# A gated mix of two attentions: row maxima of both heads in one PSUM bank, with a SyncE no-op between the halves

## The chip, the cores and the metric

The kernel runs on one core of a Trainium2 chip. The time is that of the device in microseconds (us), from launch to end; lower is better. The kernel before takes 1559.06 us (median of 3 runs, 1557.29 to 1560.24). The engines are called PE (TensorE; its weight loads, PEld, are listed apart), DVE (VectorE), ACT (ScalarE), POOL (GpSimd) and SP (SyncE).

## What is computed

Both branches read the same x of 2048 positions and 512 features, and a gate mixes them. Branch A is a dilated local attention (32 heads of 16, each position looks at 8 positions, 2 apart). Branch B is a full attention with 32 query heads and one shared head of keys and values; it is where nearly all the work is.

```python
x = A_x
g = sigmoid((x * gate_w).sum(-1, keepdims=True))
...
# branch B
q = (x @ wq).reshape(B, S, 32, 16).transpose(0, 2, 1, 3)
k = x @ wk; v = x @ wv
scores = einsum("bhqd,bkd->bhqk", q, k) * 16 ** -0.5
p = softmax(scores, axis=-1)
o = einsum("bhqk,bkd->bhqd", p, v)
b = o.transpose(0, 2, 1, 3).reshape(B, S, 512) @ wo
...
return g * a + (1 - g) * b
```

## The kernel before

**Units and steps.** Branch B is cut into 32 units: 4 blocks of 512 queries by 8 groups of 4 heads (unit u is block u // 8, group u % 8). A unit's queries stand in `qst[u % 8]`, 128 rows by 2 by 512. Rows 0 to 63 hold one head of a pair, rows 64 to 127 the other (the code's `odd` or `b`), and the middle index is the pair (`pr`). A number is kept as a high and a low part, so a head fills 48 rows; rows 62 and 63 of each half are for a shift. The keys `kst` are laid out the same way. TensorE runs a matmul on one half of its rows beside one on the other half if each writes its own PSUM bank.

**Two passes over the scores.** The softmax needs each query's row maximum before the exponential.

- *Maxima* (`max_mm`, L251): 128 queries are the stationary operand, 512 keys the moving one, and VectorE takes the maximum over the keys into the unit's tile `mx`. `fill_pair` (L269) does both heads of a pair: two matmuls into the two banks of `pm` (`m2` in the code) and one reduction of 128x1024. `fill_one` (L278) does one head alone: one matmul into the single bank `ps` (`m1`) and one reduction of 128x512 (L285). A unit needs 64 head pieces of 512 keys. When the last is in, `filled` (L258) reduces `mx` twice more and transposes the result (`mt`), ScalarE makes its high part (`shift_a`), VectorE the low part (`shift_c`, the tile `ml`), and `shift_b` (L301) writes them to rows 62 and 63 of `qst` by eight small DMAs: all eight from SyncE while branch A's pieces last, four from SyncE and four from GpSimd after that.
- *Exponentials* (`exp_pair`, L311): 128 keys are stationary, 512 queries moving; both heads of a pair go to the two banks of `pe`, and ScalarE takes the exponential of 128x1024 (`pexp`, L318). There are two such bank pairs, `eb[0]` and `eb[1]`, one for each pair of heads. The shift rows make the subtraction of the maximum part of the matmul. `weighted` (L323) then multiplies by the values: four matmuls of 32 columns each (8 in the trace) accumulate in `po` over the unit's 16 key blocks.

**The main loop** (L737) has 512 steps, 16 a unit. In each it issues the two score pairs of this step, the weighted sum of the step before, and, as far as there is room, maxima of later units: a pair into `pm` between the two score pairs and a lone piece into `ps` behind the second (the list `order`, L752). At a unit's end `finish_a` (L334) transposes `po` on VectorE and hands the scaling to GpSimd.

**The order is written out by a planner.** All instructions are issued in program order. The code keeps modelled clocks (`clk`) of TensorE, ScalarE and VectorE with fixed costs (L42: 0.23 us for a matmul pair, 0.92 for an exponential, 1.14 and 0.61 for the reductions, 1.18 for a weighted sum) and the time at which each bank comes free (`free`). `fill_ready` (L559) issues a maxima piece only if its bank is free by that clock, 0.15 us of slack allowed. `pause` (L569) fills the exponentials' banks where a unit's maxima are short. `tasks` holds later work with a due time, `run_tasks` (L598) issues what is due. Branch A's GpSimd work comes from `run_pool` (L655) in pieces with due times, with its own list `hooks` for the few VectorE and ScalarE instructions that belong to them.

**Around it.** Ahead of the loop (to 316 us) come the projections, with maxima filled in between. Four times the loop stops for an output phase (`out_phase`, L512), the product with the output weights for a quarter of the positions; it interleaves maxima as well and stores by `out_store` (L494). SyncE does no computing. It issues the queries' loads (`stack`, L228), the shift rows, loads of weights and the output stores, in the order of the program.

Of the kernel before, what the change touches and what calls it, by code (L numbers as in the profile page):

```python
# [6 lines left out]
F32 = mybir.dt.float32  # L7
# [29 lines left out]
NB = 8  # L37
NS = NU * NJ
NF = 2 * NU * 2 * 4 * 4


T_R, T_LAT, T_EXP, T_RED2, T_RED1, T_W, T_LUMP, T_Q = 0.23, 0.20, 0.92, 1.14, 0.61, 1.18, 2.53, 3.2  # L42


@with_exitstack
def gated_mix_kernel(ctx, tc, xt, wa, wk, wq, wo_a, wo_b, out):
# [191 lines left out]
    half = []  # L238
    free = {"m2": 0.0, "m1": 0.0, "e0": 0.0, "e1": 0.0, "po": 0.0}
    tasks, shifted = [], set()  # L240

    def fillable():
        return bool(half) or bool(slots) and slots[0][0] < len(stacked) and stacked[slots[0][0]] <= clk["pe"]

    def unit_tile(v):
        if v not in mx:
            mx[v] = wp.tile([P, 2, 2, 4, 4], F32, name="mx", bufs=3)
            left[v] = NF // NU
        return mx[v]

    def max_mm(dst, v, pr, t, kc, odd):  # L251
        b = 64 * odd
        nc.tensor.matmul(dst, qst[v % NB][b:b + 62, pr, t * P:(t + 1) * P], kst[b:b + 62, kc * 512:(kc + 1) * 512], start=True, stop=True)  # L253

    def to_go():
        return 2 * len(slots) + len(half)

    def filled(v, n):  # L258
        left[v] -= n
        if not left[v]:  # L260
            ms = wp.tile([P, 2, 2, 8], F32, name="ms")
            m = mx.pop(v).rearrange("p b i t k -> p b (i t) k")
            for x in range(2):
                nc.vector.tensor_reduce(ms[:, :, x, :], m, AX.X, ALU.max)
            mt = wp.tile([P, 32], F32, name="mt")
            nc.vector.transpose(mt, ms.rearrange("p b x y -> p (b x y)"))
            tasks.append((after("dve", 0, 0.5) + 0.1, shift_a, (v, mt)))

    def fill_pair(dst, key):  # L269
        v, pr, t, kc = slots.pop(0)  # L270
        m = unit_tile(v)
        for odd in range(2):
            max_mm(dst[:, odd, :], v, pr, t, kc, odd)
        nc.vector.tensor_reduce(m[:, :, pr, t, kc], dst, AX.X, ALU.max)  # L274
        free[key] = after("dve", after("pe", 0, T_R) + T_LAT, T_RED2) + 0.08
        filled(v, 2)

    def fill_one(dst=m1, key="m1"):  # L278
        if not half:
            v, pr, t, kc = slots.pop(0)  # L280
            half.extend([(v, pr, t, kc, 0), (v, pr, t, kc, 1)])
        v, pr, t, kc, odd = half.pop(0)
        m = unit_tile(v)
        max_mm(dst, v, pr, t, kc, odd)
        nc.vector.tensor_reduce(m[:, odd, pr, t, kc:kc + 1], dst, AX.X, ALU.max)  # L285
        free[key] = after("dve", after("pe", 0, T_R) + T_LAT, T_RED1) + 0.08
        filled(v, 1)

    def shift_a(v, mt):
# [5 lines left out]

    def shift_c(v, mt, th, ml):
        nc.vector.scalar_tensor_tensor(ml, mt, mk[:, 5:6], th.bitcast(F32), op0=ALU.mult, op1=ALU.add)  # L297
        after("dve", 0, 0.2)
        shift_b(v, ml)

    def shift_b(v, ml):  # L301
        for b in range(2):
# [36 lines left out]
    def finish_b(u, tt, eng):  # L339
        qb, hg = divmod(u, NHG)  # L340
        rl = wp.tile([P, 4 * 4], F32, name="rl")
        nc.vector.reciprocal(rl, tt[:, :, 16])  # L342
        at = after("dve", clk["pe"] + T_LAT, 0.8)
# [215 lines left out]
    def fill_ready(key, slack):  # L559
        if fillable() and free[key] <= clk["pe"] + slack:  # L560
            clk["pe"] = max(clk["pe"], free[key])
            if key == "m1":
                fill_one()
            elif half and (not slots or half[0][0] < slots[0][0] or slots[0][0] >= len(stacked)):
                fill_one(m2[:, 0, :], "m2")
            elif slots:
                fill_pair(m2, "m2")

    def pause(most):  # L569
        n = 0  # L570
        while n < most and slots and fillable():
            key = min(("e0", "e1", "m2"), key=lambda k: free[k])
            clk["pe"] = max(clk["pe"], free[key])
            if half:
# [20 lines left out]
            mm()  # L595
        return post

    def run_tasks():  # L598
        for task in [t for t in tasks if t[0] <= clk["pe"]]:
            tasks.remove(task)  # L600
# [37 lines left out]
    split_x(3, nc.gpsimd)  # L638
    load_wa(0)

    hooks, pool, done = [], 0.0, set()
    QK, AV = 12500, 22500
    pieces = [("load", 0)]
    wos = []
# [10 lines left out]
    def run_pool():  # L655
        nonlocal pool
        now = clk["pe"] * 1e3
        while pieces and pool < now + 3000:
# [7 lines left out]
            if kind == "load":  # L666
                a_load(g)
                pool += 500 if g else 6000
            elif kind == "qk0":
                a_scores(g, 0)  # L670
                pool += QK
            elif kind == "qk1":
                a_scores(g, 1)
                pool += QK
                hooks.append((pool + 6000, a_max, g, "max"))
            elif kind == "sub":
                a_sub(g)
                pool += 800
                hooks.append((pool + 4000, a_exp, g, "exp"))
                hooks.append((pool + 6500, a_sum, g, "sum"))  # L680
# [7 lines left out]
        for h in sorted(hooks, key=lambda h: h[0]):  # L688
            if h[0] <= now:
                hooks.remove(h)  # L690
                h[1](h[2])
                done.add((h[3], h[2]))


    lumps += [("q", m) for m in range(2, 4 * NQB)]
# [41 lines left out]
    for s in range(NS + 1):  # L737
# [100 lines left out]
```

## Time and profile before

| | |
|---|---|
| median of 3 runs | 1559.06 us (1557.29 to 1560.24) |
| the profiled execution's own time | 1558.8 us |
| its span, first to last instruction | 1557.0 us |
| granted TensorE clock | 0.998 |
| first and last exponential of the main loop | 316 and 1545 us |

The rows of the profile read so: a group has its line, engine, operation, names of what is written and read, shapes and count, then busy us and the mean ns of one, then the engine's idle time before it and who ended it. A row of a timeline has start and duration in us, engine, line, operation, names, shapes and count; in square brackets idle time before it and what released it. L253 is `max_mm` wherever it is called from, so its rows are told apart by the bank: pm, ps, pe, po, or pl in the front. L316 is a score matmul, L318 an exponential, L326 a weighted sum. Matmuls overlap: their starts are exact, their ends are modelled, so distances are taken from start to start.

### The profile page before, as it was taken

What the parts mean: (1) busy time and instruction counts of PE and PEld (TensorE: products, weight loads), DVE (VectorE), ACT (ScalarE), POOL (GpSimd) and SP (SyncE); (2) the same over time, 40 slices, a digit from 0 to 9 for tenths busy, and PEclk for the clock granted to TensorE, in tenths of its full rate; (3) what the DMA queues carried; (4) which work ended last, traced back from release to release, by engine and by line L of the source; (5) the groups of instructions that cost most, each with busy time, mean ns of one, the idle gap of its engine ahead of it and who ended that gap; (6) DMA issues with size and microseconds to landing.
All of it is one profiled execution on the core that took longest, in us unless ns stands there. A gap on an engine that the chain in (4) does not pass through costs nothing.

```text
span 1557.0 us, 25703 instructions
## 1 busy us (share of the span) xinstructions
PE 1525.7 (98%) x10076; PEld 703.8 (45%) x10076; DVE 1335.8 (86%) x1667; ACT 1120.9 (72%) x1315; POOL 834.2 (54%) x1015
## 2 busy tenths in 40 slices
PE   8999999999999999999999999999999999999998
PEld 4677777733333333333333333363354336333532
DVE  6899999979888898888899889898898889888731
ACT  4223111189999899999989998939966993999676
POOL 7420897778987898889887885240031004000210
PEclk9999999999999999999999999999999999999999
DMA  7842312211011101211111010000000000000000
GB/s 240 261 141 90 120 62 91 99 59 41 21 49 49 56 19 50 65 47 34 50 49 56 20 48 12 22 28 12 12 19 21 12 2 29 2 2 1 2 1 27
DMA packets 42889, 78.61 MB, mean 50 GB/s; under 512 B 8544, under 2 KB 25024, under 8 KB 40720
## 3 DMA queue, kind: packets, MB, share of 16 engines
q1 hardware_dynamic: 20224, 35.56, 7.9%
q0 software_dynamic: 4640, 26.99, 5.0%
q10 hardware_dynamic: 17904, 14.42, 2.8%
q8 instruction: 79, 1.29, 0.3%
q14 instruction: 42, 0.34, 0.1%
HBM read 46.96 MB, written 29.45 MB: 49 GB/s over the span
## 4 chain that ended last, share of the span: by engine, by line
PE 82%; DVE 12%; ACT 4%; issue 1%; DMA 0%; DVEq 0%; POOL 0%; ACTq 0%
PE po L326 30%; PE pe L316 21%; PE pm L253 9%; PE ps L253 8%; DVE mx L274 7%; PE pe L529 5%; DVE mx L285 4%; ACT pexp L318 3%; PE pl L159 3%; PE pl L160 2%; PE pl L161 2%; PE pl L167 1%; PE pl L253 1%; DVE ml L297 0%; PE po L253 0%
## 5 line engine op out<-in xcount | busy, mean ns | idle before, releaser
L318 ACT ACTIVATE pexp<-pe 128x1024 f32<-128x1024 f32 x1022 | 989.2, 1022 | 105.2 <-PE pe L316 100.4
L274 DVE TENSOR_REDUCE mx<-pm 128x2 f32<-128x1024 f32 x610 | 743.9, 1219 | 144.3 <-PE pm L253 140.9
L326 PE MATMUL po<-pexp,vst 128*32 128x512 f32 x4088 | 545.3, 605 | 0.7 <-ACT pexp L318 0.6
L316 PE MATMUL pe<-qst,kst 64*128 64x512 f32 x2044 | 467.0, 452 | 11.1 <-ACT pexp L318 5.8
L316 PEld LDWEIGHTS pe<-qst,kst 64*128 64x128 f32 x2044 | 191.1, 184 | 518.4 <-ACT pexp L318 506.2
L285 DVE TENSOR_REDUCE mx<-ps 128x1 f32<-128x512 f32 x597 | 405.5, 679 | 0.0
L253 PE MATMUL pm<-kst,qst 62*128 62x512 f32 x1230 | 262.6, 417 | 0.8 <-DVE mx L274 0.2
L253 PE MATMUL ps<-kst,qst 62*128 62x512 f32 x597 | 242.6, 406 | 0.4
L381 POOL TENSOR_TENSOR pr<-aext 128x512 f32<-128x512 f32 x128 | 163.9, 1302 | 57.1 <-DMA aext<-ad 57.0
L326 PEld LDWEIGHTS po<-pexp,vst 128*32 128x32 f32 x4088 | 80.4, 108 | 176.4 <-issue 163.3
L206 ACT ACTIVATE stage<-pl 128x384 f32<-128x384 f32 x64 | 31.5, 492 | 165.3 <-PE pl L161 162.8
L426 POOL TENSOR_TENSOR oa<-oa,av 128x512 f32<-128x512 f32 x112 | 143.5, 1281 | 8.8
L346 POOL TENSOR_TENSOR rl<-rl,gate_t 128x16 f32<-128x16 f32 x31 | 6.8, 220 | 242.6 <-DVE rl L342 242.6
L253 PEld LDWEIGHTS pm<-kst,qst 62*128 62x128 f32 x1230 | 117.4, 186 | 41.4 <-DVE mx L274 17.2
L253 PEld LDWEIGHTS ps<-kst,qst 62*128 62x128 f32 x597 | 111.1, 186 | 30.4 <-DVE mx L285 22.3
L424 POOL TENSOR_TENSOR av<-aext,lg 128x512 f32<-128x512 f32 x112 | 118.9, 1061 | 7.5
L305 POOL DMA_DIRECT2D qst<-ml x48 | 27.3, 573 | 134.6 <-DVE ml L297 130.8
L159 PE MATMUL pl<-wah,xh 128*128 128x384 f32 (+1 forms) x256 | 93.7, 366 | 0.4 <-ACT stage L206 0.4
L274 DVE TENSOR_REDUCE mx<-pl 128x2 f32<-128x1024 f32 x75 | 91.1, 1215 | 0.0
L160 PE MATMUL pl<-wal,xh 128*128 128x384 f32 (+1 forms) x256 | 87.1, 340 | 0.0
L161 PE MATMUL pl<-wah,xl 128*128 128x384 f32 (+1 forms) x256 | 86.9, 339 | 0.0
L529 PE MATMUL pe<-woh,turned 64*128 64x512 f32 x496 | 84.3, 400 | 0.1
(124 smaller groups left out, 1204.4 us busy)
## 6 DMA issues: line engine op xcount, KB each, us to landing
aext<-ad POOLq DMA_DIRECT2D x16, 1440.0 KB, 6.2
qst<-qd SPq DMA_DIRECT2D x64, 192.0 KB
ad<-stage ACTq DMA_DIRECT2D x32, 384.0 KB
qd<-qhi SPq DMA_DIRECT2D x32, 256.0 KB
xraw<-xt SPq DMA_DIRECT2D x16, 256.0 KB
qd<-qlo SPq DMA_DIRECT2D x16, 256.0 KB
qst<-ml SPq DMA_DIRECT2D x208, 2.0 KB
out<-two SPq DMA_DIRECT2D x12, 256.0 KB
```

The costliest lines, as they stand in the source:

```text
L159: mms.append(lambda c=c: nc.tensor.matmul(out_ap, ah(c), bh(c), start=(c == 0), stop=False))
L160: mms.append(lambda c=c: nc.tensor.matmul(out_ap, ah(c), bl(c), start=False, stop=False))
L253: nc.tensor.matmul(dst, qst[v % NB][b:b + 62, pr, t * P:(t + 1) * P], kst[b:b + 62, kc * 512:(kc + 1) * 512], start=True, stop=True)
L274: nc.vector.tensor_reduce(m[:, :, pr, t, kc], dst, AX.X, ALU.max)
L285: nc.vector.tensor_reduce(m[:, odd, pr, t, kc:kc + 1], dst, AX.X, ALU.max)
L316: nc.tensor.matmul(bank[:, odd, :], kst[b:b + 64, kt * P:(kt + 1) * P], qst[u % NB][b:b + 64, pr, :], start=True, stop=True)
L318: nc.scalar.activation(e, bank, AF.Exp, scale=SCALE)
L326: nc.tensor.matmul(po[32 * i:32 * i + 32, :], vst[:, kt, :], pexp[s, i // 2][:, i % 2, :], start=(kt == 0), stop=(kt == NJ - 1))
L381: nc.gpsimd.tensor_mul(pr[:, k], q, e[:, o:o + NJ, AC:2 * AC])
L424: nc.gpsimd.tensor_mul(av, e[:, o:o + NJ, 2 * AC:].rearrange("p j (h d) -> p j h d", d=DH), lg[:, w].unsqueeze(3).to_broadcast([P, NJ, AG, ...
L426: nc.gpsimd.tensor_add(ao, ao, av)
L529: nc.tensor.matmul(eb[x % 2][:, b, :], st[h], mv[h], start=first, stop=last)
```

## The change

- `fill_two` takes the place of `fill_one` in the main loop. It takes 256 keys for both heads of a pair (`quarter`, half of a slot). The odd head's matmul of 256 columns goes to the upper half of the bank `m1`, then SyncE gets a no-op that reads that half, then the step's two score pairs are issued, then the even head's matmul to the lower half. The second half is ordered behind the no-op, and the no-op behind the first half. One reduction of 128x512 takes both heads' maxima.
- The maxima tile has 8 columns of 256 keys where it had 4 of 512; `fill_pair` and `fill_one` reduce to two columns per head.
- The pair into `m2` is issued behind both score pairs, no longer between them, with 0.9 us of slack where there was 0.15.
- A leftover half slot goes to a free bank pair by `fill_apart`.
- The last reductions of a unit (`close`) become a task, `shift_b` a task of its own behind `shift_c`, and branch A's hooks become tasks. In the main loop at most one of the small VectorE tasks is issued per step, and none if VectorE's modelled clock is over 0.6 us ahead of TensorE's.
- `out_store` issues its store from GpSimd in place of SyncE. The planner's costs change in three places (1.18 to 1.21 for a weighted sum, 0.8 to 0.96 for `finish_a`, a new 0.14 for a 256-column pair); `mx` has two buffers, not three.

```diff
@@ -235,43 +236,45 @@
...
-            mx[v] = wp.tile([P, 2, 2, 4, 4], F32, name="mx", bufs=3)
+            mx[v] = wp.tile([P, 2, 2, 4, 8], F32, name="mx", bufs=2)
...
-    def max_mm(dst, v, pr, t, kc, odd):
-        b = 64 * odd
-        nc.tensor.matmul(dst, qst[v % NB][b:b + 62, pr, t * P:(t + 1) * P], kst[b:b + 62, kc * 512:(kc + 1) * 512], start=True, stop=True)
+    def max_mm(dst, v, pr, t, kc, odd, k=0, n=512):
+        b, k = 64 * odd, 512 * kc + k
+        nc.tensor.matmul(dst, qst[v % NB][b:b + 62, pr, t * P:(t + 1) * P], kst[b:b + 62, k:k + n], start=True, stop=True)
...
     def filled(v, n):
         left[v] -= n
         if not left[v]:
-            ms = wp.tile([P, 2, 2, 8], F32, name="ms")
-            m = mx.pop(v).rearrange("p b i t k -> p b (i t) k")
-            for x in range(2):
-                nc.vector.tensor_reduce(ms[:, :, x, :], m, AX.X, ALU.max)
-            mt = wp.tile([P, 32], F32, name="mt")
-            nc.vector.transpose(mt, ms.rearrange("p b x y -> p (b x y)"))
-            tasks.append((after("dve", 0, 0.5) + 0.1, shift_a, (v, mt)))
+            tasks.append((clk["dve"], close, (v, mx.pop(v).rearrange("p b i t k -> p b (i t) k"))))
+
+    def close(v, m):
+        ms = wp.tile([P, 2, 2, 8], F32, name="ms")
+        for x in range(2):
+            nc.vector.tensor_reduce(ms[:, :, x, :], m, AX.X, ALU.max)
+        mt = wp.tile([P, 32], F32, name="mt")
+        nc.vector.transpose(mt, ms.rearrange("p b x y -> p (b x y)"))
+        tasks.append((after("dve", clk["pe"], 0.66) + 0.1, shift_a, (v, mt)))
...
     def fill_pair(dst, key):
...
-        nc.vector.tensor_reduce(m[:, :, pr, t, kc], dst, AX.X, ALU.max)
+        nc.vector.tensor_reduce(m[:, :, pr, t, 2 * kc:2 * kc + 2], dst.rearrange("p o (h n) -> p o h n", h=2), AX.X, ALU.max)
...
@@ -282,8 +285,33 @@
...
+        nc.vector.tensor_reduce(m[:, odd, pr, t, 2 * kc:2 * kc + 2], dst.rearrange("p (h n) -> p h n", h=2), AX.X, ALU.max)
...
+        filled(v, 1)
+
+    def fill_two(between):
+
+        if not quarter:
+            v, pr, t, kc = slots.pop(0)
+            quarter.extend([(v, pr, t, kc, 0), (v, pr, t, kc, 1)])
+        v, pr, t, kc, h = quarter.pop(0)
+        m = unit_tile(v)
+        max_mm(m1[:, 256:512], v, pr, t, kc, 1, 256 * h, 256)
+        nc.sync.keepalive_nop([nc.sync.lower_ap(m1[:, 256:512])])
+        between()
+        max_mm(m1[:, 0:256], v, pr, t, kc, 0, 256 * h, 256)
+        nc.vector.tensor_reduce(m[:, :, pr, t, 2 * kc + h], m1.rearrange("p (o n) -> p o n", o=2), AX.X, ALU.max)
+        free["m1"] = after("dve", after("pe", 0, T_Z) + T_LAT, T_RED1) + 0.08
+        filled(v, 1)
+
+    def fill_apart(bank, key):
+
+        v, pr, t, kc, h = quarter.pop(0)
+        m = unit_tile(v)
+        for odd in range(2):
+            max_mm(bank[:, odd, 0:256], v, pr, t, kc, odd, 256 * h, 256)
+        nc.vector.tensor_reduce(m[:, :, pr, t, 2 * kc + h], bank[:, :, 0:256], AX.X, ALU.max)
+        free[key] = after("dve", after("pe", 0, T_Z) + T_LAT, T_RED1) + 0.08
...
@@ -295,8 +323,7 @@
 
     def shift_c(v, mt, th, ml):
         nc.vector.scalar_tensor_tensor(ml, mt, mk[:, 5:6], th.bitcast(F32), op0=ALU.mult, op1=ALU.add)
-        after("dve", 0, 0.2)
-        shift_b(v, ml)
+        tasks.append((after("dve", clk["pe"], 0.45) + 0.5, shift_b, (v, ml)))
 
@@ -498,7 +525,7 @@
         free[f"e{k}"] = after("act", clk["pe"] + T_LAT, 0.92)
         if n == C:
             nc.gpsimd.tensor_add(two[:, 0], two[:, 0], two[:, 1])
-            nc.sync.dma_start(out[0].rearrange("(p j) d -> p j d", j=NJ)[:, j, :], two[:, 0])
+            nc.gpsimd.dma_start(out[0].rearrange("(p j) d -> p j d", j=NJ)[:, j, :], two[:, 0])
         else:
             x = len(parts)
             if x < 2:
@@ -595,10 +628,18 @@
...
-    def run_tasks():
+    def run_tasks(spread=False):
+
         for task in [t for t in tasks if t[0] <= clk["pe"]]:
+            small = task[1] in (close, shift_c, finish_c, a_max, a_sum)
+            if small and spread == 2 or spread and small and clk["dve"] > clk["pe"] + BEHIND:
+                continue
             tasks.remove(task)
...
+            if small:
+                spread = spread and 2
+            if len(task) > 3:
+                done.add(task[3])
...
@@ -744,37 +780,39 @@
...
-        v = min(x[0][0] for x in (half, slots, [(NU,)]) if x)
+        v = min(x[0][0] for x in (half, quarter, slots, [(NU,)]) if x)
...
-        order = (0, "m2", 1, "m1") if s > 1 else (1, "m2", 0, "m1") if s else ()
+        order = (0, 1) if s > 1 else (1, 0) if s else ()
...
-                order = (1, "m2", 0, "m1")
+                order = (1, 0)
...
-        for which in order:
-            if which == "m2":
-                fill_ready("m2", 0.15)
-            elif which == "m1":
-                ahead = 2 * (16 * (NU - 2) - 8 - s) + 11 * (NJ - 4 - outs)
-                if ahead < to_go() - NF // NU or s >= 16 * (NU - 2) - 8 and ahead + 64 < to_go():
-                    fill_ready("m1", 0.15)
-            elif s < NS:
-                exp_pair(s, which)
+        ahead = 2 * (16 * (NU - 2) - 8 - s) + 11 * (NJ - 4 - outs)
+        more = ahead < to_go() - NF // NU or s >= 16 * (NU - 2) - 8 and ahead + 64 < to_go()
+        if more and order and s < NS and (quarter or slots) and not half and fillable() and free["m1"] <= clk["pe"] + 0.35:
+            clk["pe"] = max(clk["pe"], free["m1"])
+            fill_two(lambda: [exp_pair(s, k) for k in order])
+        else:
+            if more and half:
+                fill_ready("m1", 0.35)
+            for k in order if s < NS else ():
+                exp_pair(s, k)
+        fill_ready("m2", 0.9)
...
-        run_tasks()
+        run_tasks(True)
...
-    assert not slots and not half and not hooks and not tasks and outs == NJ, (len(slots), len(hooks), len(tasks), outs)
+    assert not slots and not half and not quarter and not tasks and outs == NJ, (len(slots), len(tasks), outs)
...
```

More of the change, by code (lines that the diff above doesn't have):

```diff
@@ L39 @@
 NF = 2 * NU * 2 * 4 * 4
-T_R, T_LAT, T_EXP, T_RED2, T_RED1, T_W, T_LUMP, T_Q = 0.23, 0.20, 0.92, 1.14, 0.61, 1.18, 2.53, 3.2
+BEHIND = 0.6
+T_R, T_LAT, T_EXP, T_RED2, T_RED1, T_W, T_LUMP, T_Q, T_Z = 0.23, 0.20, 0.92, 1.14, 0.61, 1.21, 2.53, 3.2, 0.14
 @with_exitstack
@@ L237, in gated_mix_kernel @@
     slots += [(v, pr, t, kc) for v in range(2, NU) for pr in range(2) for t in range(4) for kc in range(4)]
-    half = []
+    half, quarter = [], []
     free = {"m2": 0.0, "m1": 0.0, "e0": 0.0, "e1": 0.0, "po": 0.0}
@@ L242, in fillable @@
     def fillable():
-        return bool(half) or bool(slots) and slots[0][0] < len(stacked) and stacked[slots[0][0]] <= clk["pe"]
+        return bool(half or quarter) or bool(slots) and slots[0][0] < len(stacked) and stacked[slots[0][0]] <= clk["pe"]
     def unit_tile(v):
         if v not in mx:
-            mx[v] = wp.tile([P, 2, 2, 4, 4], F32, name="mx", bufs=3)
+            mx[v] = wp.tile([P, 2, 2, 4, 8], F32, name="mx", bufs=2)
             left[v] = NF // NU
         return mx[v]
-    def max_mm(dst, v, pr, t, kc, odd):
-        b = 64 * odd
-        nc.tensor.matmul(dst, qst[v % NB][b:b + 62, pr, t * P:(t + 1) * P], kst[b:b + 62, kc * 512:(kc + 1) * 512], start=True, stop=True)
+    def max_mm(dst, v, pr, t, kc, odd, k=0, n=512):
+        b, k = 64 * odd, 512 * kc + k
+        nc.tensor.matmul(dst, qst[v % NB][b:b + 62, pr, t * P:(t + 1) * P], kst[b:b + 62, k:k + n], start=True, stop=True)
     def to_go():
-        return 2 * len(slots) + len(half)
+        return 2 * len(slots) + len(half) + len(quarter)
     def filled(v, n):
@@ L284, in fill_one @@
         max_mm(dst, v, pr, t, kc, odd)
-        nc.vector.tensor_reduce(m[:, odd, pr, t, kc:kc + 1], dst, AX.X, ALU.max)
+        nc.vector.tensor_reduce(m[:, odd, pr, t, 2 * kc:2 * kc + 2], dst.rearrange("p (h n) -> p h n", h=2), AX.X, ALU.max)
         free[key] = after("dve", after("pe", 0, T_R) + T_LAT, T_RED1) + 0.08
+        filled(v, 1)
[19 more added lines that the diff above has]
+        free[key] = after("dve", after("pe", 0, T_Z) + T_LAT, T_RED1) + 0.08
         filled(v, 1)
@@ L342, in finish_b @@
         nc.vector.reciprocal(rl, tt[:, :, 16])
-        at = after("dve", clk["pe"] + T_LAT, 0.8)
+        at = after("dve", clk["pe"] + T_LAT, 0.96)
         if hg % 2 == 0:
@@ L563, in fill_ready @@
                 fill_one()
+            elif quarter and (not slots or quarter[0][0] < slots[0][0] or slots[0][0] >= len(stacked)):
+                fill_apart(m2, "m2")
             elif half and (not slots or half[0][0] < slots[0][0] or slots[0][0] >= len(stacked)):
@@ L570, in pause @@
         n = 0
-        while n < most and slots and fillable():
+        while n < most and fillable():
             key = min(("e0", "e1", "m2"), key=lambda k: free[k])
             clk["pe"] = max(clk["pe"], free[key])
+            if quarter:
+                fill_apart({"e0": eb[0], "e1": eb[1], "m2": m2}[key], key)
+                n += 1
+                continue
             if half:
@@ L639, in gated_mix_kernel @@
     load_wa(0)
-    hooks, pool, done = [], 0.0, set()
+    pool, done = 0.0, set()
     QK, AV = 12500, 22500
@@ L674, in run_pool @@
                 pool += QK
-                hooks.append((pool + 6000, a_max, g, "max"))
+                tasks.append(((pool + 6000) / 1e3, a_max, (g,), ("max", g)))
             elif kind == "sub":
@@ L678, in run_pool @@
                 pool += 800
-                hooks.append((pool + 4000, a_exp, g, "exp"))
-                hooks.append((pool + 6500, a_sum, g, "sum"))
+                tasks.append(((pool + 4000) / 1e3, a_exp, (g,), ("exp", g)))
+                tasks.append(((pool + 6500) / 1e3, a_sum, (g,), ("sum", g)))
             elif kind == "wo":
@@ L687, in run_pool @@
                 pool += AV
[L688 to L692, printed above, removed]
     lumps += [("q", m) for m in range(2, 4 * NQB)]
```

1 line of the change is left out of this document (added).

## The prediction

> **What bounds the kernel now.** I read the page first (engine shares and costliest groups), then the timeline of TensorE, ScalarE and the SyncE queue inside single steps, then counts by stretch.
>
> ```profile
> PE 1525.7 (98%) x10076; PEld 703.8 (45%) x10076; DVE 1335.8 (86%) x1667; ACT 1120.9 (72%) x1315; POOL 834.2 (54%) x1015
> L253 PE MATMUL pm<-kst,qst 62*128 62x512 f32 x1230 | 262.6, 417 | 0.8 <-DVE mx L274 0.2
> L253 PE MATMUL ps<-kst,qst 62*128 62x512 f32 x597 | 242.6, 406 | 0.4
> ```
>
> TensorE is busy throughout. The 615 pairs into pm cost 0.427 us a pair, hardly more than the 0.406 of one lone ps matmul: two halves of the array run side by side, and a lone one leaves half the array empty. That is the waste which the change is about. What it can be worth is decided inside a step; here are two ordinary ones, TensorE first, then ScalarE, then one weight load.
>
> ```profile
> 709.95 0.50 PE L316 MATMUL pe<-qst,kst 64*128 64x512 f32 x2
> 710.29 0.40 PE L253 MATMUL pm<-kst,qst 62*128 62x512 f32 x2
> 710.53 0.40 PE L316 MATMUL pe<-qst,kst 64*128 64x512 f32 x2
> 710.77 0.39 PE L253 MATMUL ps<-kst,qst 62*128 62x512 f32 x1
> 711.09 1.07 PE L326 MATMUL po<-pexp,vst 128*32 128x512 f32 x8
> 712.09 0.50 PE L316 MATMUL pe<-qst,kst 64*128 64x512 f32 x2
> ...
> 714.22 0.50 PE L316 MATMUL pe<-qst,kst 64*128 64x512 f32 x2
> ```
>
> ```profile
> 710.55 1.94 ACT L318 ACTIVATE pexp<-pe 128x1024 f32<-128x1024 f32 x2 [0.19 <-PE pe L316]
> ```
>
> ```profile
> 710.41 0.19 PEld L316 LDWEIGHTS pe<-qst,kst 64*128 64x128 f32 x2 [0.16 <-ACT pexp L318]
> ```
>
> A step is 2.135 us (709.95 to 714.22, two steps). Call E0 and E1 its two score pairs. From start to start: E0 to the maxima pair 0.34, to E1 0.24, to the lone ps 0.24, to the weighted sum 0.32, and 1.00 to the next E0. A pair whose weight load was not ahead of it costs 0.34 (0.50 on its row), otherwise 0.24. The exponentials start 0.60 after E0 and both end 1.94 later, at 712.49; the next E1 comes at 712.66 by the same offsets, 0.17 later. So TensorE sets this step, but ScalarE is close behind. Two kinds of step with fewer maxima show the second limit, which decides my forecast:
>
> ```profile
> 1437.20 0.51 PE L316 MATMUL pe<-qst,kst 64*128 64x512 f32 x2
> 1437.53 0.41 PE L253 MATMUL pm<-kst,qst 62*128 62x512 f32 x2
> 1437.90 0.50 PE L316 MATMUL pe<-qst,kst 64*128 64x512 f32 x2
> ...
> 1439.33 0.50 PE L316 MATMUL pe<-qst,kst 64*128 64x512 f32 x2
> ...
> 1441.22 0.50 PE L316 MATMUL pe<-qst,kst 64*128 64x512 f32 x2
> ```
>
> ```profile
> 1508.19 0.49 PE L316 MATMUL pe<-qst,kst 64*128 64x512 f32 x2
> 1508.89 0.49 PE L316 MATMUL pe<-qst,kst 64*128 64x512 f32 x2 [0.21 <-ACT pexp L318]
> 1509.31 1.06 PE L326 MATMUL po<-pexp,vst 128*32 128x512 f32 x8
> 1510.31 0.96 PE L316 MATMUL pe<-qst,kst 64*128 64x512 f32 x4
> ...
> 1512.20 0.49 PE L316 MATMUL pe<-qst,kst 64*128 64x512 f32 x2
> 1512.90 0.49 PE L316 MATMUL pe<-qst,kst 64*128 64x512 f32 x2 [0.20 <-ACT pexp L318]
> ```
>
> ```profile
> 1510.91 3.85 ACT L318 ACTIVATE pexp<-pe 128x1024 f32<-128x1024 f32 x4 [0.18 <-PE pe L316]
> ```
>
> With no maxima at all, two steps take 4.01 (1508.19 to 1512.20); with a pm pair between E0 and E1 they take 4.02. The pair is free, because E1 waits anyway: its bank is still being read by the last step's second exponential. The loop closes over two steps: E1 at 1508.89, next E0 1.42 later, exponentials 0.60 after that, 1.94 for both, and 0.05 to the E1 that this frees, at 1512.90: **1.42 + 0.60 + 1.94 + 0.05 = 4.01**. Whatever TensorE does between E0 and E1 is hidden in it. Whatever it does between E1 and the next step's exponentials lengthens it.
>
> **The change, part by part.** *Order in a step.* The pm pair and half of the new single-bank piece move from the free place to the dear one, behind E1; the other half goes ahead of E0. Behind E1 come 256 columns (half of a 0.24 slot, 0.12) and the pair (0.24), +0.36. Ahead of E0, the odd half runs on the rows that E0's odd matmul needs, so E0's result and the exponentials are later: 0.12 at most if it runs as half a slot, nothing if it hides in the exposed load; I take 0.12, as the two share rows. Loop: 4.01 + 0.36 + 0.12 = 4.49, **2.245 a step** (2.185 with the lower end), against 2.135. A load's row bears on the 0.12: E1's load started at 710.41 and its pair at 710.53, while the pair on the same rows (710.29) was in flight, so loads hide behind work on their own rows. The Trainium skill, TensorE: Matmul & The Clock Gate, section "The mechanism", says that weight loads overlap matmuls in flight only when the row group differs; by that rule E0's odd load would start only after the new half, the step would be some 0.05 longer and the sum some 23 us higher. The trace disagrees, so I leave it out.
>
> The count of steps with such a piece, from VectorE's reductions of ps outside the four output phases, and the steps in the longest stretch, from the matmuls into po, 8 a step (columns: stretch, its length, busy us, count):
>
> ```profile
> 316.50:1008.00 691.50, 211.30 (x312) 1.00 0.13 41
> 1045.00:1146.00 101.00, 31.24 (x46) 1.00 0.06 16
> 1184.00:1282.00 98.00, 30.55 (x45) 1.00 0.03 8
> 1322.00:1456.00 134.00, 33.95 (x50) 1.00 0.01 1
> ```
>
> ```profile
> 316.50:1008.00 691.50, 339.66 (x2544) 1.00 0.13 41
> ```
>
> 312 + 46 + 45 + 50 = 453 steps. 453 x 0.11 = **+50 us**. Steps with a pm pair alone go from 2.01 to (4.02 + 0.24) / 2 = 2.13; the last stretch below has a dozen (some 62 steps of 2.135 in its 134 us, 50 pieces): +1.
>
> *The no-op as a wait.* TensorE's last half waits for SyncE, which waits for the first half. Behind that half stand the pm pair, the weighted sum and the next E0, so ScalarE and VectorE wait too. No row shows the no-op; the nearest are these.
>
> ```profile
> L305 SPq DMA_DIRECT2D qst<-ml x208: 598/611/917, 114.4 to 1497.2; - x104
> L305 POOL DMA_DIRECT2D qst<-ml x48: 563/563/657, 985.9 to 1497.2; - x48
> L305 SPq EVENT_SEMAPHORE  x32: 17/17/17, 92.3 to 1444.1; - x32
> ```
>
> ```profile
> 744.97 1.36 DVE L297 SCALAR_TENSOR_TENSOR ml<-mt,mk,mh 128x32 fp32r<-128x32 f32 x1
> 746.25 1.21 DVE L274 TENSOR_REDUCE mx<-pm 128x2 f32<-128x1024 f32 x1
> 747.39 0.67 DVE L285 TENSOR_REDUCE mx<-ps 128x1 f32<-128x512 f32 x1
> ```
>
> ```profile
> 746.36 5.22 SPq L305 DMA_DIRECT2D qst<-ml  x8
> ```
>
> ```profile
> 1119.80 2.60 SPq L305 DMA_DIRECT2D qst<-ml  x4
> ```
>
> SyncE answers VectorE within 0.03 (746.33 to 746.36). The first half is done 0.50 - 0.12 = 0.38 after the step's start, the no-op takes 0.02 if it is like the semaphore instruction it most resembles and 0.61 if like a DMA issue, and TensorE goes on 0.05 later: at 0.48 or 1.07. Its turn comes 0.34 behind E1, whose bank is free at 0.72 + 1.94 + 0.05 = 2.71 of the step before, so at 2.71 - 2.245 = 0.47: 0.81. So nothing, or at most +0.26 a step; I take nothing, since it issues no descriptors.
>
> *The queue it stands in.* SyncE also issues the shift rows, eight DMAs a unit (5.22 us) while branch A lasts, four (2.60) after. The new order issues them in a later step than the multiply-add that makes ml, right behind one step's no-op and ahead of the next one's. The piece can be read some 0.26 after its slot (as the exponentials start 0.60 after E0, whose slot is 0.34): 0.81 + 0.12 + 0.26 = 1.19. Its reduction (0.67) and the pair's (1.21) last till 3.07, 0.82 into the next step; ml follows at once, or after up to 1.36 as on its row. The next no-op is due at 2.245 + 0.81 = 3.05 on that scale, so between 2.2 and 0.9 us hide. I take 1.8, as an ml that needn't wait is short. Stall: 5.22 + 0.1 - 1.8 = 3.5 and 2.60 + 0.1 - 1.8 = 0.9. How often:
>
> ```profile
> L305 SPq DMA_DIRECT2D qst<-ml x111: 610/611/917, 315.9 to 942.5; - x111
> ```
>
> ```profile
> L305 SPq DMA_DIRECT2D qst<-ml x40: 610/611/636, 985.2 to 1395.4; - x40
> ```
>
> 111 issues are 13 groups of eight and the tail of one; 40 are 10 of four. 13 x 3.5 + 10 x 0.9 = **+54 us**; bounds 0 (if all of it finds cover) and 13 x 5.3 + 10 x 2.7 = 96 (if none does). After each stall one E1 wait of about 0.12 falls away: -3.
>
> *Small pieces one a step.* The 318 steps of the longest stretch (2544 / 8) take 2.174 on average against 2.135: 0.039 x 453 = 18 us go to longer steps. If VectorE's bursts make them, spreading can save them all, otherwise none; half, **-9**. *Wider mx:* two more reductions' worth of 64 elements a unit, hidden but in the first stretch: +1. *Output stores on POOL:* twelve issues of 0.56. This stretch has the first output phase:
>
> ```profile
> 1000.00:1100.00 100.00, 98.30 (x741) 47.09 (x739) 89.99 (x108) 71.05 (x80) 21.44 (x24) 1.00 0.07 20
> ```
>
> The fifth busy time is POOL's: 21 of 100 us. So 0, and 7 us at most without that cover. Later VectorE pieces can delay POOL's branch A; it is over by 985.9, when the shift rows first go by POOL, and output phases come after it; 0, and a few us if they must wait for it.
>
> **Sum**, against the profiled run's 1558.8 (span 1557.0; 0.3 under the median 1559.06): 1558.8 + 50 + 1 + 54 - 3 - 9 + 1 = **1653**.
>
> **Rivals.**
> *Faster: the halves side by side shorten TensorE's step and nothing else binds.* Start to start 0.34 (E0), 0.24 (E1), 0.12 (second half), 0.32 (pair to weighted sum), 1.00: 2.02, or -0.115 x 453 = -52; with the -9 and +1, 1499. For it speaks that TensorE, 98% busy, was the limit. The Trainium skill, TensorEngine Tiling (Array Packing), section "Key Properties", says that tiles work independently; the trace shows it for equal lengths alone. Against it stands the loop: it decides as long as E1's bank is freed later than TensorE arrives. Freed at 0.72 + 1.94 + 0.05 - T, reached at 0.34: no wait only from T = 2.37 on. The 4.01 rows contradict it. 10%.
> *The loop alone: the DMAs find cover, for instance steps without a piece behind them.* 1653 - 54 + 3 = 1602, and down to 1575 with the loop's lower end. 19%.
> *Not side by side: 256 beside 512 columns go in lockstep, so the change doesn't do what it says.* Both halves cost a whole slot: loop 4.01 + 0.24 + 0.24 + 0.24 = 4.73, 2.365 a step, 453 x 0.12 = +54: 1707. Against: nothing but the equal-length rows. 9%.
> *No change*, by terms that cancel: 2%.
> My forecast has 60%, its own range 1600 to 1695 (lower end of the loop, -27, or half the stalls hidden; at the top stalls of 96).
>
> **Range and chances.** 1575 to 1715 holds the forecast, the loop alone and most of the lockstep case, leaving out the faster one: about 8 in 10. Faster by over 0.2% (3 us, about what can be told from no change) 10%, within 2%, slower 88%.
>
> **What would show it.** After the change a step's E1 should carry waits on pexp in most steps, and full steps should measure 2.2 to 2.3. Twenty-odd steps should be 0.9 to 3.5 longer, TensorE waiting for SyncE with eight or four L305-type DMAs just before it. ScalarE's busy time should stay near 1121. Wrong: full steps of 2.0 with no wait at E1 (the loop is broken somewhere), SyncE's no-op as the last release in every step, or shift DMAs that end before the next no-op is due.

## The result, and the profile after

The changed kernel takes **1688.94 us** (median of 4 runs, 1685.78 to 1693.70) against 1558.32 before (also of 4 runs): 1.084 times as long (95% interval 1.0811 to 1.0867). The forecast was 1653 in a range of 1575 to 1715. The profiled execution took 1685.78, its span is 1684.0.

The page of the changed kernel, for the lines that answer to those shown of before:

```profile
PE 1596.4 (95%) x10534; PEld 790.3 (47%) x10534; DVE 1338.7 (79%) x1663; ACT 1122.4 (67%) x1315; POOL 839.8 (50%) x1027
...
L254 PE MATMUL ps<-kst,qst 62*128 62x256 f32 (+1 forms) x1044 | 367.9, 352 | 52.0 <-SPq L300 49.7
```

The work of VectorE, ScalarE and GpSimd is what it was. TensorE's busy time is 71 us longer though it streams no more columns, and it waits 49.7 us for line 300, the no-op. Two ordinary steps, TensorE and then ScalarE:

```profile
894.59 0.38 PE L254 MATMUL ps<-kst,qst 62*128 62x256 f32 x1
894.60 0.91 PE L343 MATMUL pe<-qst,kst 64*128 64x512 f32 x4
895.35 0.28 PE L254 MATMUL ps<-kst,qst 62*128 62x256 f32 x1
895.36 0.50 PE L254 MATMUL pm<-kst,qst 62*128 62x512 f32 x2
895.79 1.06 PE L353 MATMUL po<-pexp,vst 128*32 128x512 f32 x8
896.79 0.38 PE L254 MATMUL ps<-kst,qst 62*128 62x256 f32 x1
896.79 1.01 PE L343 MATMUL pe<-qst,kst 64*128 64x512 f32 x4
897.64 0.28 PE L254 MATMUL ps<-kst,qst 62*128 62x256 f32 x1
...
899.07 0.38 PE L254 MATMUL ps<-kst,qst 62*128 62x256 f32 x1
```

```profile
897.51 1.94 ACT L345 ACTIVATE pexp<-pe 128x1024 f32<-128x1024 f32 x2 [0.26 <-PE pe L343]
```

```profile
897.30 0.19 PEld L343 LDWEIGHTS pe<-qst,kst 64*128 64x128 f32 x2 [0.22 <-ACT pexp L345]
```

The two steps take 4.48 us, 2.24 each; over all pairs of consecutive full steps the median is 4.49, where it was 4.27. The exponentials start 0.72 after the step's start (896.79 to 897.51), where they started 0.60 after it. The weights of the second score pair are loaded 0.51 into the step, after a wait for pexp: its bank is freed late. Before, that load waited for pexp too (0.16, at 710.41), but the maxima pair in flight covered it. Now no maxima stand there, and the score pair itself is late: it starts 0.34 into a step whose bank is free in time, and 0.51 into this one.

Then there are steps like this one, at a unit's shift rows (TensorE, then SyncE, then the granted clock by stretch: the column behind POOL's busy time is PEclk):

```profile
928.59 0.38 PE L254 MATMUL ps<-kst,qst 62*128 62x256 f32 x1
928.59 1.02 PE L343 MATMUL pe<-qst,kst 64*128 64x512 f32 x4
932.99 0.38 PE L254 MATMUL ps<-kst,qst 62*128 62x256 f32 x1 [3.38 <-SPq L300]
933.00 0.70 PE L254 MATMUL pm<-kst,qst 62*128 62x512 f32 x2
933.63 1.93 PE L353 MATMUL po<-pexp,vst 128*32 128x512 f32 x8
935.50 0.58 PE L254 MATMUL ps<-kst,qst 62*128 62x256 f32 x1
...
937.08 1.06 PE L353 MATMUL po<-pexp,vst 128*32 128x512 f32 x8
938.08 0.38 PE L254 MATMUL ps<-kst,qst 62*128 62x256 f32 x1
```

```profile
927.30 5.58 SPq L332 DMA_DIRECT2D qst<-ml  x8
```

```profile
920.00:926.60 6.60, 6.59 (x49) 2.69 (x48) 5.93 (x10) 5.89 (x8) 1.65 (x4) 1.00 0.63 231
926.60:933.00 6.40, 3.02 (x22) 1.25 (x21) 2.49 (x4) 4.40 (x6) 5.55 (x5) 1.00 0.11 39
933.00:936.40 3.40, 3.40 (x16) 1.39 (x18) 1.82 (x2) 0.00 (x0) 3.24 (x5) 0.55 0.00 1
936.40:940.00 3.60, 3.60 (x30) 1.57 (x27) 2.58 (x4) 3.15 (x4) 3.29 (x6) 0.95 0.00 0
```

SyncE issues eight shift DMAs from 927.30 to 932.88; only then comes the no-op, and the second half starts at 932.99, 4.40 into its step. After the wait the granted clock is 0.55 for some 3.4 us: the weighted sum's eight matmuls take 1.93 in place of 1.06.

Where the time went, counted step by step in the traces (a full step has a pair and a lone or split piece in it; spread is the run below in which the shift rows go two a step):

| us | before | after | spread |
|---|---|---|---|
| full steps up to 2.75 | 455, mean 2.169 | 417, mean 2.264 | 450, mean 2.269 |
| full steps over 2.75 | none | 35, sum 162.8 | 2, sum 6.0 |
| other steps | 49, sum 97.5 | 52, sum 108.6 | 52, sum 108.6 |
| four output phases | 136.8 | 136.1 | 136.1 |

The 35 long steps are 83 us above 35 usual ones of 2.27. In 14 of them eight shift DMAs stand ahead of the no-op, and the second half comes 3.7 us late on average, 51 us in all; 13 more are the steps just behind such a one, at the lower clock, and the other eight take 2.8 to 2.9. The rest of the difference is in the usual steps.

### The profile page after: what moved, and what is told of

The parts are those of the page before. It is cut to its first block, busy times and chain, and to the rows that moved or that the text cites. A ratio compares the mean times of both kernels' runs of the same rounds, so it can differ in the third digit from the quotient of the medians.

```text
span 1684.0 us, 27525 instructions
## 1 busy us (share of the span) xinstructions
PE 1596.4 (95%) x10534; PEld 790.3 (47%) x10534; DVE 1338.7 (79%) x1663; ACT 1122.4 (67%) x1315; POOL 839.8 (50%) x1027
## 4 chain that ended last, share of the span: by engine, by line
PE 67%; DVE 6%; ACT 5%; POOL 5%; SPq 5%; issue 2%; DMA 1%; DVEq 0%; ACTq 0%; POOLq 0%
PE po L353 26%; PE pe L343 15%; PE ps L254 11%; PE pm L254 8%; ACT pexp L345 5%; PE pe L556 5%; SPq L332 5%; DVE mx L277 3%; POOL pr L408 2%; DVE mx L303 1%; POOL tr L413 1%; DMA aext<-ad 1%; PE pl L160 1%; DVE ml L325 1%; PE pl L161 1%
## 5 line engine op out<-in xcount | busy, mean ns | idle before, releaser
L277 DVE TENSOR_REDUCE mx<-pm 128x4 f32<-128x1024 f32 x615 | 746.8, 1214 | 42.6 <-PE pm L254 41.5
L353 PE MATMUL po<-pexp,vst 128*32 128x512 f32 x4088 | 562.1, 623 | 2.2 <-ACT pexp L345 0.6
L343 PE MATMUL pe<-qst,kst 64*128 64x512 f32 x2044 | 493.1, 467 | 12.0 <-ACT pexp L345 5.0
L303 DVE TENSOR_REDUCE mx<-ps 128x2 f32<-128x512 f32 x450 | 308.8, 686 | 226.3 <-PE ps L254 221.5
L254 PEld LDWEIGHTS ps<-kst,qst 62*128 62x128 f32 x1044 | 196.4, 188 | 475.9 <-DVE mx L303 356.9
L254 PE MATMUL ps<-kst,qst 62*128 62x256 f32 (+1 forms) x1044 | 367.9, 352 | 52.0 <-SPq L300 49.7
L254 PE MATMUL pm<-kst,qst 62*128 62x512 f32 (+1 forms) x1246 | 310.1, 441 | 1.9 <-DVE mx L277 0.8
L343 PEld LDWEIGHTS pe<-qst,kst 64*128 64x128 f32 x2044 | 238.5, 188 | 139.7 <-ACT pexp L345 117.3
L254 PEld LDWEIGHTS pm<-kst,qst 62*128 62x128 f32 x1246 | 156.8, 189 | 55.9 <-DVE mx L277 19.9
L288 DVE TENSOR_REDUCE mx<-ps 128x2 f32<-128x512 f32 x144 | 97.8, 679 | 1.4 <-PE ps L254 1.4
L277 DVE TENSOR_REDUCE mx<-pl 128x4 f32<-128x1024 f32 x74 | 89.7, 1213 | 0.0
```

The source lines that it names most:

```text
L277: nc.vector.tensor_reduce(m[:, :, pr, t, 2 * kc:2 * kc + 2], dst.rearrange("p o (h n) -> p o h n", h=2), AX.X, ALU.max)
L303: nc.vector.tensor_reduce(m[:, :, pr, t, 2 * kc + h], m1.rearrange("p (o n) -> p o n", o=2), AX.X, ALU.max)
L343: nc.tensor.matmul(bank[:, odd, :], kst[b:b + 64, kt * P:(kt + 1) * P], qst[u % NB][b:b + 64, pr, :], start=True, stop=True)
L353: nc.tensor.matmul(po[32 * i:32 * i + 32, :], vst[:, kt, :], pexp[s, i // 2][:, i % 2, :], start=(kt == 0), stop=(kt == NJ - 1))
```

## The experiments

Theory: two things add up, the longer loop over ScalarE (order of the step) and SyncE's queue ahead of the no-op. Rivals: TensorE's own work is longer; VectorE's bank order makes the step; the long steps come from the shift chain, not from the queue.

**Shift rows by GpSimd** (changed kernel):

```diff
-                (nc.gpsimd if b and not pieces else nc.sync).dma_start(dst...
+                nc.gpsimd.dma_start(dst...
```

> The changed kernel with one edit: all shift rows are issued by GpSimd, none by SyncE, so that nothing stands in SyncE's queue ahead of the no-op but the queries' loads and the weights. If the queue makes the long steps (14 of 5.6 to 8.2 us, and some 20 of 2.75 to 3.7 behind them or later), they go, the granted clock in the stretches from 300 to 1100 us rises from 0.95 to 1.00 and the time falls by 75 to 85 us, to about 1605 to 1615. GpSimd gets some 104 more issues of 0.56 us, 58 us, in a stage in which it is about 70% busy: hidden, or up to 20 us back. Rival: the long steps come from the shift chain itself (VectorE's ml, the landing of the rows), then they stay and the time stays at 1680 to 1690.

Measured: 1660.31 us, 1.0645 of before (1.0629 to 1.0662), 29 less than the change, not 80. TensorE's waits for the no-op are gone, and the long steps fall from 35 to 11 (28 us above usual). But this edit had a price of its own. The stage ahead of the loop, whose shift rows it moved as well, is 27 us longer (the loop's first exponential starts at 338.9, in the change at 312.4). And in nine of the 11 long steps TensorE waits for ScalarE, which stands behind an exponential of branch A until GpSimd, now with the rows to issue, is done:

```profile
547.52 0.42 ACT L433 ACTIVATE lg<-lg 128x256 f32<-128x256 f32 x1 [4.46 <-POOL lg L429]
```

Such waits come to 21.9 us from the loop's start to 1200 us, and to none in the change. So this run speaks for the queue but does not settle its size; the next one does.

**Shift rows two a step** (changed kernel, main loop only):

```diff
-    def shift_b(v, ml):
-        for b in range(2):
+    def shift_b(v, ml, first=0):
+        most = 2 if looping else 8
+        for k in range(first, first + most):
+            b, g = divmod(k, 4)
...
+        if first + most < 8:
+            tasks.append((clk["pe"] + 0.1, shift_b, (v, ml, first + most)))
...
```

> The changed kernel with one edit: in the main loop a unit's shift rows are issued two per step in four steps, not all at once. Two issues take 1.3 us and fit between one step's no-op and the next one's. If SyncE's queue makes the long steps of the changed kernel (35 steps over 2.75 us, 83 us above the usual step), they go, the granted clock in the loop stays at 1.00 and the time falls by 75 to 85 us, to 1604 to 1614; full steps stay at 2.25 to 2.28. Rival: the long steps come from work that the shift rows wait for, then the time stays over 1670.

Measured: 1609.23 us, 1.033 of before (1.0314 to 1.0345). As the queue theory said, in size too: 80 us come back. The waits for the no-op, first of the changed kernel, then of this one:

```profile
L300 SPq EVENT_SEMAPHORE  x450: 17/17/28, 312.6 to 1528.6; - x150
...
  PEld ps L254: 56.7, 21
  PE ps L254: 49.7, 17
```

```profile
L300 SPq EVENT_SEMAPHORE  x450: 17/17/28, 316.7 to 1452.3; - x150
...
  PEld ps L254: 2.0, 3
  PE ps L254: 0.9, 1
```

The same 450 no-ops of 17 ns each cost 57 us of waiting (by the weight loads' rows, PEld) in one order of SyncE's queue and 2 in the other. The granted clock over the span goes from 0.977 back to 0.998. What is left, 52 us above before, is the order of the step, but for some 4 us of the rest of the change (last run).

**The no-op alone** (kernel before; the pair's reduction, and so the next pair, waits for SyncE):

```diff
             max_mm(dst[:, odd, :], v, pr, t, kc, odd)
+        if noop:
+            nc.sync.keepalive_nop([nc.sync.lower_ap(dst[:, 1, 0:256])])
...
-                fill_pair(m2, "m2")
+                fill_pair(m2, "m2", True)
```

> The kernel before with one addition: in the main loop SyncE gets a no-op that reads the pair's bank, so that the next step's pair waits for SyncE. Order, pieces and reductions are as before. If the no-op is as short as a semaphore instruction and costs only where SyncE is busy with shift rows (and with its wait for ml, which here stands in the queue as well), full steps stay at 2.13, some 13 steps get 3 to 6 us longer and a dozen more 1 to 3, and TensorE then runs some us at half clock: 60 to 110 us in all, 1620 to 1670. Rival: it costs in every step (2.2 or more), or it costs nothing (1558).

Measured: 1690.84 us, 1.0852 of before (1.0836 to 1.0869): 133 us, more than the 110 that I expected at most. The median full step is still 2.13; 29 long steps are 124 us above it, up to 10.0 us long. Here SyncE reaches the shift rows before ml is made, and VectorE's next instruction behind ml is the reduction that waits for the no-op, so nothing hides the 5.2 us of issues. One such step, SyncE, VectorE and TensorE:

```profile
807.71 5.22 SPq L307 DMA_DIRECT2D qst<-ml  x8
```

```profile
807.25 0.43 DVE L299 SCALAR_TENSOR_TENSOR ml<-mt,mk,mh 128x32 fp32r<-128x32 f32 x1
813.15 1.23 DVE L276 TENSOR_REDUCE mx<-pm 128x2 f32<-128x1024 f32 x1 [5.47 <-SPq L275]
```

```profile
809.09 0.51 PE L318 MATMUL pe<-qst,kst 64*128 64x512 f32 x2
814.43 0.80 PE L253 MATMUL pm<-kst,qst 62*128 62x512 f32 x2 [4.84 <-DVE mx L276]
```

ml is done at 807.68, the issues end at 812.93, and only behind them comes the no-op (line 275). VectorE's reduction waits 5.47 for it, and the next pair stands behind the reduction, which gives its bank back at 814.38. So the one queue reaches TensorE through a second engine, with the reduction's 1.23 on top. In the usual step the no-op costs TensorE nothing; with the shift rows ahead of it in the queue it costs as much as the whole change.

**Both pieces behind the second score pair**, lone piece first, then in a second run pair first (kernel before):

```diff
-        order = (0, "m2", 1, "m1") if s > 1 else ...
+        order = (0, 1, "m1", "m2") if s > 1 else ...     (first run)
+        order = (0, 1, "m2", "m1") if s > 1 else ...     (second run)
```

> The kernel before with one edit: in each step the lone piece and the pair are both issued behind the second score pair; no half pieces, no no-op, no spreading. If the loop over ScalarE sets the step (bank free, second score pair, what stands behind it, weighted sum, exponentials), a full step goes from 2.135 to (4.01 + 0.48) / 2 = 2.245 us, with waits on pexp at the second pair, and the time rises by about 50 us to 1600 to 1612. Rival: TensorE's own work sets the step, then the order in it does not matter, steps stay at 2.13 to 2.15 and the time within 5 us of 1558.

> The kernel before with pair and lone piece both behind the second score pair as in the run before, but the pair first, so that VectorE reduces the pair first and its bank comes free early. TensorE's work and the loop over ScalarE are the same as with the lone piece first. If the loop over ScalarE sets the step, full steps are again 2.245 and the second score pair waits for pexp. If it was VectorE, which gives back the pair's bank last (0.70 into the next step, where the pair was due at 0.76), steps go back to 2.13 to 2.17 and the time to 1560 to 1580.

Measured: 1662.32 us, 1.0658 of before (1.0644 to 1.0673), and 1615.04, 1.0368 (1.035 to 1.0385). Full steps have a median of 2.28 and 2.27, against 2.133 and the 2.245 expected. Two steps of the second run:

```profile
881.84 0.91 PE L316 MATMUL pe<-qst,kst 64*128 64x512 f32 x4
882.59 0.40 PE L253 MATMUL pm<-kst,qst 62*128 62x512 f32 x2
882.83 0.39 PE L253 MATMUL ps<-kst,qst 62*128 62x512 f32 x1
...
884.15 0.78 PE L316 MATMUL pe<-qst,kst 64*128 64x512 f32 x4
...
886.33 0.50 PE L316 MATMUL pe<-qst,kst 64*128 64x512 f32 x2
```

Together 4.49, as in the loop's formula (4.01 + 0.48), with the same matmuls as before in another order. Over all pairs of consecutive full steps the median is 4.49 as well, the same as in the change and in the spread run, where other matmuls stand in the step. With the pair first VectorE gives its bank back early, and the step is as long: the loop over ScalarE is enough by itself. (No run changed the length of the exponentials, so the loop is shown by this sum and by the order, not by a faster ScalarE.) That the first run took 104 us in place of 50 has another cause: in 44 steps a lone piece was issued but no pair, as the pair's bank was late by the planner's clock, and maxima ran short. The loop had to stop for them twice, in steps of 19 us, and eight long steps add 34, the longest of them with a wait of 10.3 us of TensorE for the shift rows to land.

**Reductions in the other order** (kernel before; TensorE's order unchanged):

```diff
+        red = lambda: nc.vector.tensor_reduce(m[:, :, pr, t, kc], dst, AX.X, ALU.max)
+        if later and left[v] > 3:
+            late.append(red)
...
+        while late:
+            late.pop(0)()
```

> The kernel before with one edit: TensorE's order is as before (pair between the score pairs, lone piece behind them), but VectorE reduces the lone piece first and the pair after it. If the pair's bank closes a loop over VectorE (lone piece readable 1.24 into the step, its reduction 0.61, the pair's 1.21, 0.05 to TensorE, which wants the bank again 0.34 into a step), a full step takes 1.24 + 0.61 + 1.21 + 0.05 - 0.34 = 2.77 and the time rises by some 280 us, to 1800 to 1860. Rival: VectorE is idle for 14% of the span, so the order of its two reductions costs nothing or little, under 1580.

Measured: 1866.48 us, 1.1982 of before (1.1958 to 1.2006), full steps 2.886 (median), just over what I expected. VectorE, idle for 28% of this run's span, closes a loop of its own (TensorE, then VectorE):

```profile
908.47 0.50 PE L322 MATMUL pe<-qst,kst 64*128 64x512 f32 x2
909.46 0.50 PE L253 MATMUL pm<-kst,qst 62*128 62x512 f32 x2 [0.49 <-DVE mx L276]
...
910.03 0.40 PE L253 MATMUL ps<-kst,qst 62*128 62x512 f32 x1
...
912.35 0.50 PE L253 MATMUL pm<-kst,qst 62*128 62x512 f32 x2 [0.48 <-DVE mx L276]
```

```profile
910.47 0.69 DVE L291 TENSOR_REDUCE mx<-ps 128x1 f32<-128x512 f32 x1 [1.06 <-PE ps L253]
911.08 1.22 DVE L276 TENSOR_REDUCE mx<-pm 128x2 f32<-128x1024 f32 x1
```

From pair to lone piece 0.57, 0.44 until it can be read, 0.61 and 1.22 for the reductions, 0.05 back: 2.89. I had 2.77; most of the difference is that the pair, once it waits, loads its weights in the open (0.34 to the score pair behind it, not 0.24).

**First half behind the first score pair** (changed kernel):

```diff
+        between[0]()
         max_mm(m1[:, 256:512], v, pr, t, kc, 1, 256 * h, 256)
         nc.sync.keepalive_nop([nc.sync.lower_ap(m1[:, 256:512])])
-        between()
+        between[1]()
...
```

> The changed kernel with one edit: the first half of the single-bank piece is issued behind the step's first score pair, no longer ahead of it. The first exponential then starts 0.60 after the step's start, not 0.71. If the first half costs its 0.11 in the loop, full steps go from 2.24 on average to 2.185, and the time falls by 20 to 30 us, to 1660 to 1668. Rival: TensorE's own length sets the step, as the matmuls are the same: no change within 5 us of 1688. If the wait for the no-op then binds, the time rises instead.

Measured: 1700.47 us, 1.0906 of before (1.089 to 1.0922), 12 above the change. The saving that I expected failed to come; what came is the last sentence of the expectation, the wait for the no-op. The exponentials do start at 0.60 again, but the time isn't saved: usual full steps have a median of 2.253 (2.274 in the change) and a mean of 2.281 (2.264). A weight load shows what now ends last, and a reduction what ends shortly before it:

```profile
919.19 0.18 PEld L254 LDWEIGHTS ps<-kst,qst 62*128 62x128 f32 x1 [0.18 <-SPq L301]
```

```profile
922.47 1.22 DVE L277 TENSOR_REDUCE mx<-pm 128x4 f32<-128x1024 f32 x1
```

With the first half later, the second waits 0.18 for the no-op, and not only here: 433 of its loads wait so (133.5 us in all), against 21 in the change (56.7). And the pair's reduction ends 2.95 into its step (920.74 to 923.69), so that its bank is free 0.70 into the next one, where the pair starts at 0.76 to 0.82. Without the wait for the no-op the pair's bank would be next.

**The rest of the change alone** (changed kernel with the old order, no half pieces, no no-op):

```diff
-            fill_two(lambda: [exp_pair(s, k) for k in order])
...
+        for x, k in enumerate(order):
+            if s < NS:
+                exp_pair(s, k)
+            if not x:
+                fill_ready("m2", 0.15)
+            elif more:
+                fill_ready("m1", 0.15)
```

> The changed kernel with the order of a step as before (pair between the score pairs, a lone piece of 512 keys behind them, slack 0.15), no half pieces and no no-op; all else of the change stays: wider maxima tile, VectorE's small pieces one a step, shift rows as a task of their own, output stores by GpSimd, the planner's costs. If VectorE's bursts made the longer steps (mean 2.17 against a median of 2.135), spreading saves 5 to 18 us: 1540 to 1553. Rival: it saves nothing, 1556 to 1562, or the later pieces cost more than they save, over 1562.

Measured: 1563.87 us, 1.0029 of before (1.0018 to 1.0041): slightly slower. The usual full steps are what they were (454, mean 2.168, where before had 2.169), so spreading VectorE's small pieces saves nothing. One place costs some 7 us: ScalarE (first row) stands behind an exponential of branch A until GpSimd is done, and TensorE with it.

```profile
507.21 0.42 ACT L433 ACTIVATE lg<-lg 128x256 f32<-128x256 f32 x1 [5.31 <-POOL lg L429]
```

```profile
508.59 0.80 PE L343 MATMUL pe<-qst,kst 64*128 64x512 f32 x2 [4.90 <-ACT pexp L345]
```

None of the runs beats the kernel before, and none points to a version that would: in the orders tried, the loop over ScalarE, the one over VectorE or the distance that the no-op needs makes one of the two halves dear. One obvious order was not run: the halves as in the change and the pair in its old place between the score pairs. By the loop it would take an estimated (4.01 + 0.12 + 0.12) / 2 = 2.125 a step, next to the 2.133 of before.

## Why the prediction came out as it did

The direction and both mechanisms were right. The queue's price was too small, by a part that the sum did not have. Term by term:

- *Loop, +50 and +1.* Forecast 2.245 a step; measured 4.49 for two by the median, and 2.27 on average with the disturbed ones. The spread run, which has the loop without the queue, is 52 us above before. In it 452 full steps are 0.104 longer on average, 47 us, and the other steps give 5, where I had put 50 and 1; a step with a pair alone takes the 2.13 of the forecast. The 0.12 of the first half is the move of the exponentials from 0.60 to 0.72.
- *No-op itself, 0.* Right: 17 ns, and no wait for it in the usual step.
- *Queue, +54 - 3.* The stalls' own length was right in sum, in part by luck. 14 groups of eight make the second half 3.7 us late each, 51 in all, where I had 13 of 3.5, 46; the groups of four, for which I had 9, left matmuls waiting for less than 1 in all. But the runs with and without the queue differ by 80. The other 29 come behind the stalls, where the clock is at half, as in 933.00 to 936.40 above. The 14 stalls are followed by 22 stretches of half clock of 3.4 us each, in which TensorE is busy for 69 us; at full clock that work would take some 34 us less (an estimate, and part of it is covered by waits). **This is the part that was missed: a price behind each stall.** I had counted a stall as its own length.
- *Spreading, -9; wider mx, +1; output stores, 0.* The spreading was wrong: the whole rest of the change costs 4, with one place in it that costs 7. That VectorE's bursts made the longer steps was only assumed; spreading them left the mean as it was. What makes those steps longer stays open. The wider mx and the stores were not measured apart.

Put together: without the queue I had 1602, and the spread run has 1609; for the queue I had 51, and it costs 80. The sum of 1653 is 36 short of 1689, 7 by the first and 29 by the second.

Of the rivals, the faster one falls by the length of the step, 2.24 where it had 2.02. The sign that I named for the loop, waits for pexp at the second score pair, is weak by itself: in the kernel before 894 weight loads of score pairs already waited for pexp (506 us), but ahead of time, with other matmuls in flight. The loop alone was priced at 1602; the spread run is that case. The lockstep case falls by the 0.72: a first half that took a whole slot would have put the exponentials at 0.84. So 256 columns do run beside 512 on the other rows; that saving exists, but it lies where TensorE waits anyway.

## What to carry to other kernels

Before moving work inside a step, close each loop through a shared buffer: from the instruction that waits for the buffer, through all that stands behind it, to the reader that frees it. Work in front of the waiting instruction is free up to the wait, work behind it isn't, however busy the engine looks. And an ordering wait through another engine costs what stands in that engine's queue: list its DMA issues ahead of choosing it, and spread them. Price a stall with the slow stretch behind it: here 29 us on top of 51.

## What the runs showed of the hardware

A stall of TensorE is followed by a slow stretch: after the wait of 3.38 us shown above the granted clock is 0.55 from 933.00 to 936.40, and a weighted sum takes 1.93 in place of 1.06. In the trace of the changed kernel all 14 stalls (waits of 2.71 to 4.50 us) are followed by half clock: for 3.4 us in the six cases where it began after the wait, for 6.8 in the eight where it began before the wait was over. The shortest of the waits, and the stretch of half clock behind it:

```profile
539.31 0.38 PE L254 MATMUL ps<-kst,qst 62*128 62x256 f32 x1 [2.71 <-SPq L300]
```

```profile
540.84:544.25 3.41, 3.41 (x20) 1.56 (x16) 2.53 (x3) 1.94 (x2) 3.17 (x4) 0.50 0.02 5
```

The Trainium skill, TensorE: Matmul & The Clock Gate, section "What's actually happening", states a half rate after about 3.4 us without activity, and full rate again after as long a busy window. The trace agrees in the half rate and in the busy window, but not in the time without activity: 2.71 us were enough here, and with the no-op alone six of seven waits of 2.2 to 2.6 us were followed by half clock as well. The waits of some 1.2 us at the output phases never were. I had not applied the rule, since the kernel before kept a clock of 0.998.

Small DMAs are dear for the queue that issues them: 0.61 us each with 2 KB, 5.6 for the eight shown. And two matmuls on different halves of the array need not be of the same length, or start together, to run side by side: with 256 columns ahead of the score pair's 512 on one half, the exponentials start 0.12 later, half a slot of 0.24.
